# A gated mix of attention and FFN: a new list of steps, which also says where each gelu tanh is queued

## The chip, the cores and the metric

The kernel runs on one core of a Trainium2 chip. The metric is the device time of one execution, in microseconds. Before the change the median of three runs is 1306.47 us (1300.94 to 1306.64).

## What is computed

The reference takes 2048 tokens of 512 numbers and mixes two branches by a gate per token. One branch is attention with 32 query heads of size 16 over a single key and value head; the other is an FFN with a gelu gate and 1376 hidden columns.

```python
q = (x @ wq) as 32 heads of 16;  k = x @ wk;  v = x @ wv
p = softmax(q @ k.T * 16 ** -0.5)            # per head, 2048 x 2048
a = (p @ v, heads side by side) @ wo
b = (gelu(x @ w_gate) * (x @ w_up)) @ w_down # gelu by the tanh formula
g = sigmoid((x * gate_w).sum(-1))
out = g * a + (1 - g) * b
```

All is in float32. The FFN, the projections and `wo` are computed with each operand split into a rounded high part and the rest (`split`, L196), in three products; scores take both parts of q and k side by side in 51 rows.

## The kernel before

A prologue of some 80 us loads x and the weights, projects q, k and v and writes q to DRAM in a layout that is read back by head. The rest, over nine tenths of the time, is one long list of steps for TensorE, in which attention and FFN are interleaved, and this list is written out by hand or by a planner as `PLAN` (L44): 78 lines of letters, each with a count behind it.

- **S**, a score (`scores`, L724): for a group of queries and 128 keys, two matmuls (L738) that run side by side in the two halves of the array's rows write 128 x 1024 scores into a pair of PSUM banks, and ScalarE takes the exponential of it all into a buffer `p` in SBUF (L741). There are three such bank pairs (`two_banks`, L137). S takes the one of the first two that has been unused for longer; **Z** is a score that takes the third. There are 1024 S and Z in all.
- **V**, a visit (`visit`, L818, and `pv`, L802): four matmuls (L808; eight records in a profile) multiply the two oldest pairs of `p` with v and add to an accumulator in one PSUM bank. After 16 V's the accumulator is full: VectorE copies it out (`norm`, L744, the copies are L752 and L762), which frees the bank, and the later steps of the norm are put on a list `bg` of small VectorE work. There are 512 V's.
- **H** and **F**, a job of the FFN or of `wo`: H opens the job. It takes the third bank pair for its result `z` and a bank of its own for `y`; an **F** is one pair of matmuls (L503), one for z and one for y, again in the two halves of the array's rows (`pair_mm`, L497). A job goes through its terms twice, the second time with the halves exchanged; between the two stands a small instruction on POOL, `mark` (L511), for which the second half waits. A gate job (`gate_job`, L562) computes a chunk of 128 hidden columns of gate (z) and up (y) for 512 tokens, in 24 F's; a down job (`down_job`, L590) multiplies two or three finished chunks with `w_down`, adding z and y to the output (L608, L610); a `wo` job does the same for the attention's result. Every third F (`slot`, L477) also issues one small piece of work from the lists `todo` (splits of the next weights: a cast on VectorE, L200, and a subtraction on POOL, L201), `lazy` and `bg`.
- **R** ends the job (`end`).

What follows a gate job is a chain of four links (`gelu`, L524): VectorE copies z out (`gs`, L528), then *inner*, two VectorE operations (L531, L532) that make the tanh's argument `sq`; *tanh* on ScalarE (L535); *outer* (L538, L539), two VectorE operations, the second of which reads y; *halves* (L543, L544), which split the result into `hh` and `hl` for the down job. The copy and *inner* are issued at R. The other links wait on the list `chain`, and `advance(m)` (L549) issues links until only m are left. Every engine works through its own queue in order, so a link that is issued early stands in front of what is issued later on the same engine, whether its input is there or not.

Before the change four things issue the links: the job's `end` puts them off by a number of scores (`defer`, L295, counts S and Z as they are issued; `run_later`, L655, is called by each of them ahead of its own matmuls), tanh by 3, outer by 5, halves by 6; H issues up to outer, as its y needs the old bank; the next gate job's `gelu` issues all that is left; and `ffn_jobs` (L635) issues all of it before it hands out the first down job of a batch, because that job reads `hh` and `hl`:

```python
            if r % 3 == 2 or r == NF - 1:
                flush(chain)
                batch = hold[:]
```

`play` (L827) is called for each line of the list with the next job of its kind. A job's `begin` is called first, then the letters are played one by one. `begin` of a gate job also issues the load of the weights two chunks on (`fetch_w`, L298), flushes `todo` and puts off the splits of the next chunk's weights by two scores. There are 39 gate jobs in the list, 32 down jobs in 16 batches and six `wo` jobs, with 1608 F's.

## Time and profile before

| | |
|---|---|
| median of three runs | 1306.47 us |
| the profiled execution's own time | 1303.09 us |
| its span, first to last instruction | 1301.3 us |
| mean granted TensorE clock | 0.991 |
| TensorE busy | 1260.4 us (97%) |
| ScalarE busy | 1033.5 us (79%) |
| VectorE busy | 559.7 us (43%) |
| POOL busy | 222.9 us (17%) |
| exponentials on ScalarE | 1024, 979.6 us |
| tanhs of the gelu, 128 x 512 | 40, 25.0 us |

PE is TensorE, PEld its loading of weights, DVE VectorE, ACT ScalarE. A row of a timeline gives the start in us from the span's start, the duration, the engine, the line, the operation, the tiles (written <- read), the shapes and how many equal instructions are merged; in brackets stands idle time ahead of it and what ended that. A row of the waits gives who waited for whom, the us in total, how often and the longest. Since matmuls are pipelined and overlap, their price is read from start to start.

### The profile page before, as it was taken

The page shows a single profiled execution, that of the slowest core. Times are in us where ns is not written, and L with a number is a line of the kernel's source. Part 1 is how long each engine was busy: PE and PEld are TensorE (multiplying, and loading weights), DVE is VectorE, ACT ScalarE, POOL GpSimd, SP SyncE. Part 2 cuts the span into 40 slices and gives each one's busy share as a digit, 9 for nine tenths or more (in the row PEclk, how much of TensorE's full clock was granted, in tenths as well). Part 3 has the DMA queues.
Part 4 walks back from the last instruction along what each step waited for, and adds up shares of the span by engine and source line. Part 5 has one row for each costly group of instructions (what it writes and reads, how often), then busy time and mean ns, then how long its engine had stood idle before and what let it go on. Part 6 is the DMA issues. An engine that isn't in the chain of part 4 may idle for free.

```text
span 1301.3 us, 23608 instructions
## 1 busy us (share of the span) xinstructions
PE 1260.4 (97%) x9742; PEld 653.5 (50%) x9742; DVE 559.7 (43%) x843; ACT 1033.5 (79%) x1126; POOL 222.9 (17%) x264
## 2 busy tenths in 40 slices
PE   9989999999999999999999999999999999999998
PEld 6865545454545545544454544444544554454545
DVE  6872543525523352533453244261555225254334
ACT  4547888787888888878888878897888789788884
POOL 4420312112300210202230021120231012021100
PEclk9999999999999999999999999999999999999999
DMA  8550201012200211101210211010221201011000
GB/s 315 186 176 19 79 25 59 17 46 78 70 14 18 79 38 38 63 22 38 98 38 14 71 62 38 17 60 1 73 85 38 70 14 62 25 39 38 14 1 33
DMA packets 28173, 73.89 MB, mean 57 GB/s; under 512 B 4192, under 2 KB 4192, under 8 KB 28064
## 3 DMA queue, kind: packets, MB, share of 16 engines
q1 hardware_dynamic: 27520, 71.06, 16.4%
q8 instruction: 77, 1.26, 0.4%
q0 software_dynamic: 256, 0.79, 0.2%
q10 hardware_dynamic: 288, 0.52, 0.1%
q14 instruction: 32, 0.26, 0.1%
HBM read 57.41 MB, written 14.94 MB: 56 GB/s over the span
## 4 chain that ended last, share of the span: by engine, by line
PE 88%; DVE 4%; ACT 1%; issue 1%; DMA 0%; ACTq 0%; SPq 0%; DVEq 0%
PE acc L808 36%; PE s L738 22%; PE z L503 16%; PE y L503 14%; ACT p L741 1%; DVE sq L531 1%; DVE sq L532 1%; DVE gs L528 1%; PE wos L488 1%; DVE gs L539 0%; DVE sq L538 0%; DMA Q<-scr 0%; DVE acc L620 0%; DVE nz L774 0%; ACT sq L535 0%
## 5 line engine op out<-in xcount | busy, mean ns | idle before, releaser
L741 ACT ACTIVATE p<-s 128x1024 f32<-128x1024 f32 x1024 | 979.6, 1025 | 184.3 <-PE s L738 169.4
L808 PE MATMUL acc<-p,v 128*32 128x512 f32 x4096 | 505.8, 610 | 0.0
L738 PE MATMUL s<-Q,kp 51*128 51x512 f32 x2048 | 408.7, 426 | 27.1 <-ACT p L741 25.6
L738 PEld LDWEIGHTS s<-Q,kp 51*128 51x128 f32 x2048 | 187.6, 185 | 292.6 <-ACT p L741 191.8
L808 PEld LDWEIGHTS acc<-p,v 128*32 128x32 f32 x4096 | 109.0, 110 | 236.0 <-issue 228.0
L201 POOL TENSOR_TENSOR gl<-st,gh 128x512 fp32r<-128x512 f32 x80 | 113.8, 1439 | 334.4 <-PE s L738 159.6
L503 PE MATMUL y<-xh,gh 64*128 64x512 f32 x312 | 123.5, 396 | 5.5 <-DVE gs L539 5.4
L528 DVE COPY gs<-z 128x512 f32<-128x512 f32 x39 | 27.0, 691 | 231.6 <-PE z L503 179.0
L503 PE MATMUL z<-xh,gh 64*128 64x512 f32 x312 | 123.0, 394 | 0.3 <-ACT p L741 0.3
L503 PE MATMUL z<-xl,gh 64*128 64x512 f32 x312 | 122.3, 392 | 0.0
L503 PE MATMUL y<-xl,gh 64*128 64x512 f32 x312 | 122.1, 391 | 0.0
L503 PE MATMUL z<-xh,gl 64*128 64x512 f32 x312 | 122.0, 391 | 0.0
L503 PE MATMUL y<-xh,gl 64*128 64x512 f32 x312 | 121.9, 391 | 0.0
L511 POOL MEMSET mark<- 1x1 f32 x77 | 9.0, 117 | 629.8 <-PE y L503 613.4
L610 DVE SCALAR_TENSOR_TENSOR acc<-z,gc,acc 128x512 f32<-128x512 f32 x24 | 18.0, 751 | 165.5 <-PE z L503 114.7
L503 PE MATMUL y<-dh,hh 64*128 64x512 f32 x176 | 71.5, 406 | 0.0
L503 PE MATMUL z<-dh,hh 64*128 64x512 f32 x176 | 71.5, 406 | 0.0
L503 PE MATMUL z<-dl,hh 64*128 64x512 f32 x176 | 68.8, 391 | 0.0
L503 PE MATMUL y<-dl,hh 64*128 64x512 f32 x176 | 68.8, 391 | 0.0
L503 PE MATMUL z<-dh,hl 64*128 64x512 f32 x176 | 68.8, 391 | 0.0
L503 PE MATMUL y<-dh,hl 64*128 64x512 f32 x176 | 68.8, 391 | 0.0
L201 POOL TENSOR_TENSOR dl<-st,dh 128x512 fp32r<-128x512 f32 x44 | 58.3, 1325 | 54.2 <-DVE dh L200 51.9
(167 smaller groups left out, 1576.1 us busy)
## 6 DMA issues: line engine op xcount, KB each, us to landing
st<-wf SPq DMA_DIRECT2D x40, 768.0 KB
scr<-q SPq DMA_DIRECT2D x16, 512.0 KB
Q<-scr SPq DMA_DIRECT2D x64, 128.0 KB
Q<-scr SPq DMA_DIRECT2D x64, 64.0 KB
out<-acc SPq DMA_DIRECT2D x16, 256.0 KB
xr<-xT SPq DMA_DIRECT2D x6, 512.0 KB
xst<-xT SPq DMA_DIRECT2D x12, 256.0 KB
xr<-xT SPq DMA_DIRECT2D x4, 256.0 KB
```

The costliest lines, as they stand in the source:

```text
L201: eng_l.tensor_sub(lo, src, hi)
L488: nc.tensor.matmul(ps, a, b, start=(first and q == 0), stop=(last and q == len(terms) - 1), skip_group_check=True)
L503: mm = nc.tensor.matmul(ps, a[rs], b[rs], start=(half == 0 and q == 0), stop=(half == 1 and q == len(X) - 1), skip_group_check=True)
L511: relay = nc.gpsimd.memset(mark, 0.0).ins
L528: nc.vector.tensor_copy(gs, g)
L531: nc.vector.scalar_tensor_tensor(sq, gs, GC, gs, op0=ALU.mult, op1=ALU.mult)
L532: nc.vector.scalar_tensor_tensor(sq, sq, 1.0, gs, op0=ALU.add, op1=ALU.mult)
L610: nc.vector.scalar_tensor_tensor(o, ps, w, o, op0=ALU.mult, op1=ALU.add)
L738: nc.tensor.matmul(ps[:, j * TG : (j + 1) * TG], kp[rs, kc * P : (kc + 1) * P], Q[u][rs, pr], start=True, stop=True)
L741: nc.scalar.activation(p, ps, AF.Exp, bias=0.0, scale=SCALE)
L808: nc.tensor.matmul(accp[u][32 * j : 32 * j + 32], vt[:, kc], pb[s, j // 2][:, (j % 2) * TG : (j % 2 + 1) * TG], start=(kc == 0), stop=(kc ...
```

## The change

The list has a new letter, T, and is a new list. T issues a gate job's tanh where it stands, and puts off outer and halves by two and three scores from there; the job's `end` no longer puts off anything. And each line of the list now begins at H: what stood at the head of a line of before, the scores and visits between one job and the next, now stands at the end of the line of the earlier job, behind its R. So `begin` of a job, and the flush of the chain ahead of a first down job, are played after the scores and visits of the gap, no longer ahead of them. The list holds the same 1024 scores (120 in the third bank pair, 111 before), 512 V's, 77 jobs and 1608 F's; its V's stand in 278 groups instead of 268. Nothing else in the kernel is changed.

```diff
 PLAN = [
-    "f: S2 H F5 S F5 S F2 S V S F2 S F3 S F5 S F2 R",
-    "f: S V S Z S V3 S Z S V2 H F S F3 S F3 S F2 S V S F3 S F5 S2 F R",
...
+    "t: S",
+    "f: H F S F5 S F4 S F2 S V S F2 S F4 S F4 S F2 R S V Z S T S V3 S Z S V2 S",
...
@@ -577,8 +577,6 @@
         def end(z, y):
             gelu(n, z, lambda: y)
             advance(3)()
-            for k, m in ((3, 2), (5, 1), (6, 0)):
-                defer(k, advance(m))
             if r == NF - 1:
                 flush(todo)
                 fetch_w(n + 3)
@@ -834,6 +832,10 @@
                     score(t[0] == "Z")
             elif t[0] == "V":
                 visit(k)
+            elif t[0] == "T":
+                advance(2)()
+                for k, m in ((2, 1), (3, 0)):
+                    defer(k, advance(m))
             elif t[0] == "H":
                 advance(1)()
                 z = two_banks("z", 2)[:, 0:TG]
```

The first place is on ScalarE, from the tanh of gate job 6 to the scores behind the one of gate job 8 (`sq` is the tile that a tanh turns into its result, `p` the output of an exponential). Before:

```order
L535 ACTIVATE sq_2491<-sq_2491 128x512
L741 ACTIVATE p<-s 128x1024 x15
L535 ACTIVATE sq_2669<-sq_2669 128x512
L741 ACTIVATE p<-s 128x1024 x14
L535 ACTIVATE sq_2870<-sq_2870 128x512
L741 ACTIVATE p<-s 128x1024 x40
```

And now:

```order
L535 ACTIVATE sq_2487<-sq_2487 128x512
L739 ACTIVATE p<-s 128x1024 x14
L535 ACTIVATE sq_2664<-sq_2664 128x512
L739 ACTIVATE p<-s 128x1024 x16
L535 ACTIVATE sq_2865<-sq_2865 128x512
L739 ACTIVATE p<-s 128x1024 x37
```

The third tanh of each piece is that of gate job 8, which a down job follows. 125 exponentials of the list stand ahead of the second tanh in both. Job 8's last score is the 139th of the list before and the 138th now; its tanh stood right behind the 139th exponential and now stands behind the 141st, three past the job's last score. Over all 39 gate jobs, 15 tanhs stood with no exponential between the job's last score and them, and 24 with two; now 32 stand with three, three with two and four with one, each of the four behind a group of three V's.

The second place is on TensorE, from the end of gate job 12 to the start of gate job 13 (`acc` rows are V's, 4 matmuls each, `s` rows scores, 2 matmuls each). Before:

```order
L503 MATMUL y<-xh_3605,gl_3349 128x512
L738 MATMUL s<-Q_3140,kp 128x512 x2
L808 MATMUL acc_3589<-p,v_75 32x512 x4
L738 MATMUL s<-Q_3140,kp 128x512 x4
L738 MATMUL s<-Q_3577,kp 128x512 x2
L808 MATMUL acc_3589<-p,v_75 32x512 x16
L738 MATMUL s<-Q_3577,kp 128x512 x4
L503 MATMUL z<-xh_3605,gh_3742 128x512
```

And now:

```order
L503 MATMUL y<-xh_3629,gl_3417 128x512
L736 MATMUL s<-Q_3542,kp 128x512 x2
L806 MATMUL acc_3604<-p,v_75 32x512 x4
L736 MATMUL s<-Q_3542,kp 128x512 x4
L806 MATMUL acc_3604<-p,v_75 32x512 x8
L736 MATMUL s<-Q_3542,kp 128x512 x6
L806 MATMUL acc_3972<-p,v_76 32x512 x8
L736 MATMUL s<-Q_3542,kp 128x512 x2
L503 MATMUL z<-xh_3629,gh_3813 128x512
```

Before, the last V's of an accumulator stood directly ahead of the two scores and the job; now they stand earlier, and three scores, two V's of the next accumulator and one more score come between them and the job.

The third place is on POOL, over the gate jobs 6 and 7 (`gl` and `dl` are subtractions of the next weights' splits, `mark` stands between a job's halves; the first `mark` of the piece of now belongs to two down jobs and gate job 6). Before:

```order
L511 MEMSET mark 1x1 x2
L201 TENSOR_TENSOR gl_2342<-st_1868,gh_2341 128x512 x2
L511 MEMSET mark 1x1
L201 TENSOR_TENSOR dl_2340<-st_1868,dh_2339 128x512
L201 TENSOR_TENSOR gl_2513<-st_2324,gh_2512 128x512 x2
L511 MEMSET mark 1x1
```

And now:

```order
L511 MEMSET mark 1x1 x3
L201 TENSOR_TENSOR gl_2420<-st_1964,gh_2419 128x512 x2
L201 TENSOR_TENSOR dl_2418<-st_1964,dh_2417 128x512
L511 MEMSET mark 1x1
L201 TENSOR_TENSOR gl_2576<-st_2386,gh_2575 128x512 x2
L201 TENSOR_TENSOR dl_2574<-st_2386,dh_2573 128x512
```

Two of a job's three subtractions stood ahead of its `mark` and one behind it; now all three stand behind it.

## The prediction

> **What bounds the kernel now.** I read the page first: how busy each engine is, and the chain that ended last.

> ```profile
> PE 1260.4 (97%) x9742; PEld 653.5 (50%) x9742; DVE 559.7 (43%) x843; ACT 1033.5 (79%) x1126; POOL 222.9 (17%) x264
> ...
> PE 88%; DVE 4%; ACT 1%; issue 1%; DMA 0%; ACTq 0%; SPq 0%; DVEq 0%
> ```

> TensorE is the bound, and DMA is nothing. A list that only reorders its work can change two things: what a step costs by what stands beside it, and where TensorE waits. So I read TensorE's timeline for the prices of the steps. In these rows `acc` x8 is one V, `s` x2 one score, a z and a y row one F.

> ```profile
> 110.48 0.68 PE L738 MATMUL s<-Q,kp 51*128 51x512 f32 x4
> 111.00 0.40 PE L503 MATMUL y<-dh,hl 64*128 64x512 f32 x1
> 111.00 0.40 PE L503 MATMUL z<-dh,hl 64*128 64x512 f32 x1
> 111.33 1.93 PE L808 MATMUL acc<-p,v 128*32 128x512 f32 x16
> 113.18 0.97 PE L738 MATMUL s<-Q,kp 51*128 51x512 f32 x6
> 114.08 2.78 PE L808 MATMUL acc<-p,v 128*32 128x512 f32 x24
> 116.80 0.50 PE L738 MATMUL s<-Q,kp 51*128 51x512 f32 x2
> 117.13 0.39 PE L503 MATMUL z<-dh,hh 64*128 64x512 f32 x1
> ```

> ```profile
> 127.67 0.39 PE L503 MATMUL z<-xl,gh 64*128 64x512 f32 x1
> 127.68 0.39 PE L503 MATMUL y<-xl,gh 64*128 64x512 f32 x1
> 127.91 0.45 PE L738 MATMUL s<-Q,kp 51*128 51x512 f32 x2
> 128.20 0.39 PE L503 MATMUL z<-xh,gl 64*128 64x512 f32 x1
> ```

> By starts, an F or a score takes 0.23 to 0.24 us (127.67 to 127.91). A group of V's costs more at its ends: 0.33 from the F at 111.00 to the first V, 1.85 for two V's (114.08 to 116.80 is 2.72 for three, so one more V is 0.87 and 0.11 goes at the end), and 0.33 for the first score behind (116.80 to 117.13). That is 0.10 + 0.11 + 0.10 = 0.31 a group. Laid on the whole list of before, such prices give 1136.1 us for the 1202.0 us from the first score at 82.8 to the last V at 1284.9. The other 66 us are waits, matmuls at a lower clock and scatter, and the rest of this part finds them. TensorE's own waits:

> ```profile
> PE s L738 <- ACT p L741: 25.6, 16, 1.9
> PE y L503 <- DVE gs L539: 7.1, 5, 1.7
> ```

> Scores wait 16 times for an exponential, nearly always 1.9 us. On ScalarE stands the cause:

> ```profile
> ACT sq L535 <- DVE sq L532: 24.8, 15, 1.9
> ```

> Fifteen of 39 gelu tanhs reach ScalarE's queue before their input is there. The gap after gate job 8, on TensorE, VectorE and ScalarE:

> ```profile
> 246.02 0.40 PE L738 MATMUL s<-Q,kp 51*128 51x512 f32 x2
> 246.35 1.07 PE L808 MATMUL acc<-p,v 128*32 128x512 f32 x8
> 247.35 0.73 PE L738 MATMUL s<-Q,kp 51*128 51x512 f32 x4
> 249.99 0.64 PE L738 MATMUL s<-Q,kp 51*128 51x512 f32 x2 [1.92 <-ACT p L741]
> ```

> ```profile
> 246.22 0.69 DVE L528 COPY gs<-z 128x512 f32<-128x512 f32 x1 [2.35 <-PE z L503]
> 246.95 0.69 DVE L531 SCALAR_TENSOR_TENSOR sq<-gs 128x512 f32<-128x512 f32 x1
> 247.67 0.69 DVE L532 SCALAR_TENSOR_TENSOR sq<-sq,gs 128x512 f32<-128x512 f32 x1
> ```

> ```profile
> 245.53 1.02 ACT L741 ACTIVATE p<-s 128x1024 f32<-128x1024 f32 x1
> 248.40 0.63 ACT L535 ACTIVATE sq<-sq 128x512 f32<-128x512 f32 x1 [1.85 <-DVE sq L532]
> 248.94 2.83 ACT L741 ACTIVATE p<-s 128x1024 f32<-128x1024 f32 x3
> ```

> The tanh can run at 248.40 at the earliest, but stands ahead of the exponential of the score of 246.02. ScalarE stands still for 1.85 us with three scores ready, no score bank comes free, and the score due at 247.9 (0.33 and 0.23 behind 247.35) starts at 249.99. It loses 2.08 us: 1.92 of waiting and 0.16 because its weights are no longer loaded in advance.

> A second loss follows it. The first row is the whole span's, the others give, for a stretch, its length, TensorE's busy time, the granted clock and the DMA:

> ```profile
> core 0: 1301.3 us, clock 0.991
> ```

> ```profile
> 246.00:256.00 10.00, 8.08 (x52) 0.83 0.00 0
> 559.00:569.00 10.00, 8.08 (x54) 0.83 0.00 1
> ```

> ```profile
> 256.00:559.00 303.00, 296.63 (x2404) 1.00 0.15 48
> ```

> Seven windows of 10 us (from 92, 246, 559, 680, 795, 883 and 1112) have 0.83 or so, and each holds one of those waits; between them the clock is 1.00. Each loses 0.17 of 10 us, 1.7 us. Seven make 11.9 us, and 0.009 of 1301.3 us is 11.7.

> The five waits of `y` are of another kind; here is the start of gate job 13, on VectorE and on TensorE:

> ```profile
> 351.69 0.69 DVE L752 COPY n<-acc 128x512 f32<-128x512 f32 x1 [2.59 <-PE acc L808]
> 352.30 0.68 DVE L538 SCALAR_TENSOR_TENSOR sq<-sq,gs 128x512 f32<-128x512 f32 x1
> 353.01 0.69 DVE L539 SCALAR_TENSOR_TENSOR gs<-y,sq 128x512 f32<-128x512 f32 x1
> ```

> ```profile
> 351.55 0.74 PE L738 MATMUL s<-Q,kp 51*128 51x512 f32 x4
> 352.13 0.39 PE L503 MATMUL z<-xh,gh 64*128 64x512 f32 x1
> 353.76 0.50 PE L503 MATMUL y<-xh,gh 64*128 64x512 f32 x1 [1.24 <-DVE gs L539]
> ```

> The old `y` bank is read by L539, which is queued on VectorE behind the copy of a finished accumulator, and that copy waits for the V's just ahead of the job. From 352.13 to 353.76 an F takes 1.63 instead of 0.23.

> **The change, part by part.** The sum is made against the profiled execution, 1303.1 us (span 1301.3, 1.8 around it); the median of the three timed runs, 1306.5, is 0.3% above it.

> *Where the tanh stands.* Counted in the lists and ScalarE's order, 15 tanhs of before have no exponential between the job's last score and themselves (all where a down job follows, so the chain was finished early), and 24 have two. Those 24 do not wait. Now 32 have three, three have two and four have one. In job 8's gap the first exponential can start at 246.42, when its score ends, and three at 0.94 (2.83 for three) end past 249.2; the input is ready at 248.40. The four with one follow a group of three V's: the tanh may wait, but the next score comes only some 3.3 us after the job's last F (0.23 + 0.33 + 2.7), and VectorE's chain ends 2.6 us after it (246.02 less 0.23, to 248.40). So all 15 stalls go: 25.6 of waiting and 15 times 0.16, **-28.0**.

> *The low clock.* If the stalls cause it, **-11.9**. The row first: idle of 1.92 us was enough seven times in 15. [...]

> *The `y` waits.* L538 and L539 now come two scores behind the tanh, and the list keeps at least two V's between them, or the accumulator's copy, and the next job. Two V's and their ends are some 2.1 us, the two operations 1.4. All five go: 7.1 and five times 0.16, **-7.9**.

> *Late scores.* The score at 127.91 is followed 0.29 later, not 0.23: its bank came free just too late to load weights in advance. In the whole timeline 148 of 3,129 steps are 0.04 to 0.20 late, 10.9 us in sum (the first at 83.2, the last at 1269.6). ScalarE gives an exponential per 0.94 us. By the prices, 110 scores of before start less than 2.7 us after the third score before them (third-bank scores left aside), and 11 of the new list. The ends are 0 and 10.9; I take **-8.0**, as nine tenths of the tight places go but not every late step need be one.

> *More groups of V's.* 278 against 268: ten times 0.31, **+3.1**. Every kind of matmul keeps its number.

> *What moves along, at nothing.* A job's `begin` is played at H now, no longer at the end of the job before, so its weight fetch (SP), its splits (VectorE, POOL) and the flush of `todo` come later in their queues. The fetched weights are split one job later, over 10 us on; VectorE is 43% busy and runs ahead of TensorE. On POOL three subtractions stand behind a job's `mark` where two stood ahead of it; their end is due 4 to 5 us after the job's middle, about when the job ends. If that cover fails, a chain meets them: the second rival. The loads of Q hang on scores and do not move.

> The sum: 1303.1 - 28.0 - 11.9 - 7.9 - 8.0 + 3.1 = 1250.4, rounded up to **1251 us**.

> **The rivals.** *The low-clock windows stay.* [...] Against it: the places above. 1251 + 11.9 = 1263; chance 0.07.

> *POOL holds up the gelu chain.* One row of the view of the tile `sq` (shortest, median and longest duration) speaks for it:

> ```profile
> L532 DVE SCALAR_TENSOR_TENSOR sq<-sq,gs x40: 691/692/1632, 81.8 to 1259.1; 128x512 f32<-128x512 f32 x40
> ```

> The one of 1632 ns ran against a POOL subtraction, 0.94 us too long. [...] If the later subtractions hit every chain, a tanh behind three exponentials still has its input about in time; the seven with fewer lose up to 0.94 each, 6.6 us: 1257; chance 0.08.

> *ScalarE is too tight.* With the stalls gone the same 1024 exponentials must fit in 50 us less, and the late scores stay: 1251 + 8 = 1259; chance 0.07.

> *The far side: every gate job waits for `y`.* What five jobs paid, 39 could pay, if L539, now fixed two scores behind a later tanh, came after the next H. 34 more at 1.58 us (7.9 / 5) are 53.7; with the 7.9 that then stay: 1250.4 + 61.6 = 1312, slower by 0.4% than the median and 0.7% than the profiled run. It decides where less than 1.4 us of TensorE's work lies between that place and H; I find no such gap in the list. 0.02, with 0.01 more for a partial case near no change.

> **How the numbers follow.** My case has 0.75. It is the likeliest, so 1251. Its own range is 1246 (every late step goes, 1247.5, and a little scatter) to 1257. The range reaches up over the POOL and ScalarE rivals to the low-clock windows: 1246 to 1264. About 0.5% is what a measurement of this kernel can tell from no change, 6.5 us; all cases but the last are faster by far more: 0.97, 0.01, 0.02.

> **What would show it.** In the profile of the changed kernel the wait of `sq` L535 for L532 falls from 24.8 us to under 4, TensorE's wait for `p` from 25.6 to under 3 and for L539 from 7.1 to under 1, the mean clock rises to 0.998 or more, and the page's TensorE share to 98%. A clock still at 0.991 without long waits shows the first rival; L531 or L532 medians above 692 ns the second; many waits of weight loads for `p` the third. A time above 1275 means that a wait took another's place, and my reading of the gaps is wrong.

## The result, and the profile after

| | before | after |
|---|---|---|
| median | 1306.49 us (four runs, 1300.94 to 1306.64) | 1252.9 us (four runs, 1252.69 to 1253.59) |
| the profiled execution's own time | 1303.09 us | 1252.75 us |
| its span | 1301.3 us | 1250.9 us |

The changed kernel takes 0.9601 of the time of before (95% interval 0.9575 to 0.9626). 1251.0 was predicted, 1246 to 1264 as the range.

The page of the changed kernel: how busy each engine is, and the chain that ended last. Line numbers between a gate job's `end` (L580) and the new letter in `play` are lower by two than before: L741 is L739 now, L738 is L736, L808 is L806.

```profile
PE 1239.9 (99%) x9742; PEld 657.1 (53%) x9742; DVE 519.3 (42%) x843; ACT 1032.1 (83%) x1126; POOL 214.2 (17%) x264
...
PE 92%; DVE 1%; DMA 0%; ACT 0%; issue 0%; SPq 0%; DVEq 0%
```

```profile
core 0: 1250.9 us, clock 0.999
```

TensorE went from 97% to 99% busy, with 20.5 us less of busy time for the same 9742 matmuls; about half of that is the low clock (seven stretches of 3.41 us at half clock before, one now), which the next section prices. Its longest waits now:

```profile
PE z L503 <- DVE oh L780: 3.9, 1, 3.9
PE pw L213 <- DVE kmx L214: 1.2, 1, 1.2
```

The 25.6 us for exponentials and the 7.1 us for L539 are gone from the list altogether, and at its head stands a wait that the kernel before did not have. On ScalarE the tanhs' wait fell from 24.8 us to this:

```profile
ACT sq L535 <- DVE sq L532: 3.2, 4, 1.3
```

The gap after gate job 8 once more, on VectorE, ScalarE and TensorE. It ran from 246.02 before and runs from 238.17 now:

```profile
239.82 0.69 DVE L532 SCALAR_TENSOR_TENSOR sq<-sq,gs 128x512 f32<-128x512 f32 x1
```

```profile
240.09 1.94 ACT L739 ACTIVATE p<-s 128x1024 f32<-128x1024 f32 x2 [0.41 <-PE s L736]
241.91 0.63 ACT L535 ACTIVATE sq<-sq 128x512 f32<-128x512 f32 x1
242.43 2.85 ACT L739 ACTIVATE p<-s 128x1024 f32<-128x1024 f32 x3
```

```profile
239.49 0.97 PE L736 MATMUL s<-Q,kp 51*128 51x512 f32 x6
240.38 1.92 PE L806 MATMUL acc<-p,v 128*32 128x512 f32 x16
242.24 0.73 PE L736 MATMUL s<-Q,kp 51*128 51x512 f32 x4
```

The tanh's input is ready at 240.51 (239.82 and 0.69), 2.34 us after the first score behind the job (238.17); before it was 2.34 us too (246.02 to 248.36). But now ScalarE is still at the exponentials that stand ahead of the tanh, until 241.91, so it waits for nothing, and TensorE has no idle time in the whole gap. VectorE does the same work at the same speed, 0.69 us for L528, L531 and L532 each. TensorE's order of scores and V's is the same up to the fourth score, the one that waited before, but for the bank pairs of the second and the third. What differs is the place of one 0.63 us instruction in ScalarE's queue.

### The profile page after: what moved, and what is told of

Read it like the earlier page. It is cut to its first block, busy times and chain, and to the rows that moved or that the text cites. A ratio compares the mean times of both kernels' runs of the same rounds, so it can differ in the third digit from the quotient of the medians.

```text
span 1250.9 us, 23613 instructions
## 1 busy us (share of the span) xinstructions
PE 1239.9 (99%) x9742; PEld 657.1 (53%) x9742; DVE 519.3 (42%) x843; ACT 1032.1 (83%) x1126; POOL 214.2 (17%) x264
## 4 chain that ended last, share of the span: by engine, by line
PE 92%; DVE 1%; DMA 0%; ACT 0%; issue 0%; SPq 0%; DVEq 0%
PE acc L806 38%; PE s L736 23%; PE y L503 16%; PE z L503 14%; PE wos L488 1%; DVE nz L772 0%; DVE acc L618 0%; DMA Q<-scr 0%; PE wof L488 0%; DVE sq L531 0%; DVE n L763 0%; DVE sq L532 0%; DVE nt L775 0%; DVE gs L539 0%; DVE sq L538 0%; DVE hl L544 0%
## 5 line engine op out<-in xcount | busy, mean ns | idle before, releaser
L739 ACT ACTIVATE p<-s 128x1024 f32<-128x1024 f32 x1024 | 979.3, 1025 | 156.9 <-PE s L736 149.9
L806 PE MATMUL acc<-p,v 128*32 128x512 f32 x4096 | 497.7, 600 | 0.0
L736 PE MATMUL s<-Q,kp 51*128 51x512 f32 x2048 | 396.4, 421 | 0.8 <-DMA Q<-scr 0.8
L736 PEld LDWEIGHTS s<-Q,kp 51*128 51x128 f32 x2048 | 183.1, 184 | 258.9 <-ACT p L739 157.5
L806 PEld LDWEIGHTS acc<-p,v 128*32 128x32 f32 x4096 | 107.2, 109 | 236.5 <-issue 224.5
L528 DVE COPY gs<-z 128x512 f32<-128x512 f32 x39 | 27.0, 691 | 251.2 <-PE z L503 229.7
L503 PE MATMUL z<-xh,gh 64*128 64x512 f32 x312 | 123.2, 395 | 0.0
L503 PE MATMUL y<-xh,gh 64*128 64x512 f32 x312 | 123.1, 394 | 0.0
L503 PE MATMUL y<-xl,gh 64*128 64x512 f32 x312 | 121.9, 391 | 0.0
L503 PE MATMUL y<-xh,gl 64*128 64x512 f32 x312 | 121.9, 391 | 0.0
L503 PE MATMUL z<-xh,gl 64*128 64x512 f32 x312 | 121.9, 391 | 0.0
L503 PE MATMUL z<-xl,gh 64*128 64x512 f32 x312 | 121.9, 391 | 0.0
L201 POOL TENSOR_TENSOR gl<-st,gh 128x512 fp32r<-128x512 f32 x80 | 106.9, 1354 | 63.4 <-DVE gh L200 51.2
L503 PE MATMUL y<-dh,hh 64*128 64x512 f32 x176 | 69.4, 395 | 0.0
L503 PE MATMUL z<-dh,hh 64*128 64x512 f32 x176 | 69.4, 395 | 0.0
L503 PE MATMUL y<-dl,hh 64*128 64x512 f32 x176 | 68.8, 391 | 0.0
L503 PE MATMUL y<-dh,hl 64*128 64x512 f32 x176 | 68.8, 391 | 0.0
L503 PE MATMUL z<-dh,hl 64*128 64x512 f32 x176 | 68.8, 391 | 0.0
L503 PE MATMUL z<-dl,hh 64*128 64x512 f32 x176 | 68.8, 391 | 0.0
L503 PEld LDWEIGHTS z<-xh,gh 64*128 64x128 f32 x312 | 58.0, 186 | 8.3 <-ACT p L739 1.7
```

The costliest lines, as they stand in the source:

```text
L201: eng_l.tensor_sub(lo, src, hi)
L503: mm = nc.tensor.matmul(ps, a[rs], b[rs], start=(half == 0 and q == 0), stop=(half == 1 and q == len(X) - 1), skip_group_check=True)
L528: nc.vector.tensor_copy(gs, g)
L736: nc.tensor.matmul(ps[:, j * TG : (j + 1) * TG], kp[rs, kc * P : (kc + 1) * P], Q[u][rs, pr], start=True, stop=True)
L739: nc.scalar.activation(p, ps, AF.Exp, bias=0.0, scale=SCALE)
L806: nc.tensor.matmul(accp[u][32 * j : 32 * j + 32], vt[:, kc], pb[s, j // 2][:, (j % 2) * TG : (j % 2 + 1) * TG], start=(kc == 0), stop=(kc ...
```

## Where the 50 us came from

I laid the price of each step (the prediction's 0.23 for an F or a score, 0.87 and 0.31 for V's) beside its measured length, from the start of one step of TensorE to the next, for every step of the main loop, in both profiled executions. What exceeds the price by 0.04 to 0.20 us is called late, by more long. The prices in the sums have more digits than these: with the printed ones all steps come to 1133 and 1136 us, some 3 us less in each kernel.

| us | before | after |
|---|---|---|
| prices of all steps | 1136.1 | 1139.4 |
| late steps | 161, 12.2 | 23, 2.0 |
| long steps | 42, 48.6 | 4, 5.4 |
| the rest (scatter) | 4.7 | 5.0 |
| main loop | 1202.0 | 1152.2 |

The 48.6 of before part into 27.8 at the 15 tanh stalls, 11.5 in the low clock behind them, 7.9 at the five waits for `y`, and 1.4 elsewhere. The 5.4 of after stand at one place, the new wait. The loop gives 49.8 us of the 50.3, the prologue and the end the other 0.5.

## Experiments

**The theories.** Mine is the prediction's: the gain is made by where a tanh, its followers and the flush ahead of a down job stand in their queues, 28 us directly and 12 through the clock, and late scores and V groups belong to the list's order. The rivals: the gain comes from the new order of scores and visits as such (more even for ScalarE), with the stalls only a symptom; or the stalls and the low clock are separate losses. Each expectation below gives the numbers of the theories for that run.

**The old list, cut at H.** The list of before, its lines cut anew so that each begins at H (the first lines of the edit). Not one score, visit or F changes place on TensorE; what changes is when `begin` and the flush of the chain are played. The delays are the old 3, 5 and 6.

```diff
-    "f: S2 H F5 S F5 S F2 S V S F2 S F3 S F5 S F2 R",
-    "f: S V S Z S V3 S Z S V2 H F S F3 S F3 S F2 S V S F3 S F5 S2 F R",
+    "t: S2",
+    "f: H F5 S F5 S F2 S V S F2 S F3 S F5 S F2 R S V S Z S V3 S Z S V2",
...
```

> The old list, only cut anew: each line begins at H, so no chain is finished early; links are put off by 3, 5 and 6 scores as before. Theory A (the tanh's place makes the long waits, and these make the low clock): all 39 tanhs stand behind two exponentials, ScalarE's wait for L532 falls from 24.8 us to under 2, the mean clock rises from 0.991 to 0.998 or more; the waits for y grow from 7.9 to about 13 us, since outer is now 5 scores late ahead of down jobs too: 1303.1 - 28.0 - 11.9 + 5 = 1268 us. Rival B (the gain is the new list's mix of steps): above 1295. Rival C (the low clock has another cause): clock still 0.991, about 1280.

Measured: 1266.86 us (ratio 0.9708, 0.9685 to 0.9730). The profiled execution's cores and TensorE's longest wait:

```profile
core 0: 1265.8 us, clock 0.998
```

```profile
PE y L503 <- DVE gs L539: 8.9, 7, 1.7
```

No tanh waits any more, and the clock went from 0.991 to 0.998 with them, at TensorE's old order and the old prices (1136.1). The cut alone gives 38 us (against the runs of before beside it, median 1304.67), where the change gave 54 against its own; by the ratios, 2.9% of 4.0%. The late steps hardly moved (149, 11.0 us), and the waits for `y` went from 7.1 to 8.9 us, less than I had expected. That rules out the order of scores and visits as the cause of the stalls.

**The same, with outer one score earlier.** To see whether the `y` waits are a term of their own:

```diff
-            for k, m in ((3, 2), (5, 1), (6, 0)):
+            for k, m in ((3, 2), (4, 1), (6, 0)):
```

> As e1_rotate, with outer put off by 4 scores instead of 5. Theory A: the y waits fall to some 2 us, the small late starts of the old list stay (10.9 us): 1303.1 - 28.0 - 11.9 - 6 = 1257 us, with over 100 late steps left. Rival (late starts were a consequence of the long waits): they go too, 1247 us.

Measured: 1255.34 us (ratio 0.9623, 0.9601 to 0.9644).

```profile
core 0: 1253.6 us, clock 0.999
```

```profile
PE y L503 <- DVE gs L539: 0.5, 1, 0.5
```

Seven waits became one short one, and 11.5 us went, 3.1 more than the 8.4 us of waiting. By my estimate the clock makes some 1.3 of it (0.998 against 0.999 in the two profiled runs, 0.001 of 1265.8 us), and 1.1 is the 0.16 us that the wait after gate job 8 of before lost on top of its 1.92, taken seven times; the rest stays unexplained. With one digit changed the old order of TensorE's work reaches within 2.4 us of the new list. 142 late steps, 10.5 us, are still there, now that hardly a stall is left: they belong to the old list's order, not to the stalls.

**The new list, with the old delays.** The other half: the new list without its T's, and tanh, outer and halves put off by 3, 5 and 6 scores in `end`, as before.

> The new list without T: the tanh, outer and halves are put off by 3, 5 and 6 scores from the job's end, as before the change. Theory A: two exponentials ahead of a tanh are enough, so no long waits; outer comes up to one score later than now and a few y waits return, about 4 us: 1253 + 4 = 1257 us. Rival (the third exponential ahead of the tanh is what matters): tens of tanh waits on ScalarE, 1275 us or more.

```diff
-    "f: H F S F5 S F4 S F2 S V S F2 S F4 S F4 S F2 R S V Z S T S V3 S Z S V2 S",
+    "f: H F S F5 S F4 S F2 S V S F2 S F4 S F4 S F2 R S V Z S S V3 S Z S V2 S",
...
             advance(3)()
+            for k, m in ((3, 2), (5, 1), (6, 0)):
+                defer(k, advance(m))
```

Measured: 1260.36 us (ratio 0.9665, 0.9642 to 0.9688).

```profile
PE z L503 <- DVE oh L782: 3.8, 1, 3.8
PE y L503 <- DVE gs L539: 1.7, 1, 1.7
PE s L738 <- ACT p L741: 1.4, 5, 0.3
```

Again no tanh waits: the letter T is not what frees them, the cut is. T is worth 7 us here (10.0 us of long steps against 5.4, 37 late steps against 23). I had put it 3 us too low. In place of 4 us at waits for `y` the profile has 1.9 at one such wait, 1.7 at five short waits for `p`, which I had not counted, and 1.6 more of late steps than the changed kernel.

**The changed kernel, with the early flush put back.** The gate job's `end` issues the whole chain at once where a down job follows, as before; all else is the changed kernel.

```diff
             advance(3)()
+            if r % 3 == 2 or r == NF - 1:
+                flush(chain)
```

> The new kernel, but the chain of a gate job that a down job follows is issued whole at R, as before the change; T stays for the others. Theory A: 15 or 16 tanhs wait on ScalarE again, about 25 us there; TensorE loses 22 to 28 us in scores and up to 12 by the lower clock: 1253 + 22 to 40 = 1275 to 1293 us, clock 0.991 to 0.995. Rival B (the new list is what counts): below 1262. Rival C (the clock does not follow the waits): clock 0.999.

Measured: 1284.61 us (1283.03 to 1288.53; ratio 0.9843, 0.9819 to 0.9867).

```profile
core 0: 1286.7 us, clock 0.991
```

```profile
PE s L738 <- ACT p L741: 21.8, 17, 2.3
```

```profile
ACT sq L535 <- DVE sq L532: 27.6, 16, 2.2
```

The gap after gate job 8, on ScalarE:

```profile
243.83 0.63 ACT L535 ACTIVATE sq<-sq 128x512 f32<-128x512 f32 x1 [1.79 <-DVE sq L532]
```

Everything came back that was said to go: the tanhs' waits, the scores' waits behind them, and the low clock. The 0.991 is that of the profiled run, the slowest of the four; the others have 0.993 to 0.995, still below the changed kernel's 0.999. From before over the changed kernel to this one the low clock went and came with the stalls: 0.991 where the tanhs wait 24.8 us, 0.999 where they wait 3.2, 0.991 again where they wait 27.6. The time lies 32 us above the changed kernel, and the late steps (39, 3.8 us) did not come back.

**One exponential between.** The same, but the chain put off by two scores instead of issued at once, so that one exponential or so comes between the job's last score and the tanh:

```diff
             advance(3)()
+            if r % 3 == 2 or r == NF - 1:
+                defer(2, advance(0))
```

> The new kernel, but in gate jobs that a down job follows the tanh is issued with the second score behind R, so that one exponential stands between. Theory A: ScalarE waits some 0.7 to 0.9 us in each of about 15 places, 12 to 15 us in all, but most of it is covered, since a score bank is free: TensorE loses about 3 us, the clock stays at 0.999: 1256 us. Rival (each wait of ScalarE costs TensorE about what it cost before): 1270 us or more.

Measured: 1257.82 us (ratio 0.9655, 0.9636 to 0.9673).

```profile
core 0: 1256.1 us, clock 0.997
```

```profile
ACT sq L535 <- DVE sq L532: 12.5, 15, 1.3
```

Fifteen tanhs still wait, 12.5 us in all against 27.6, but that costs only 5 us against the changed kernel: with one exponential more ahead of the tanh, ScalarE's stall of 0.8 us (12.5 in 15) mostly ends before TensorE needs a bank (its waits for `p` are 2.0 us in all). So ScalarE's 0.8 us of standing still cost TensorE little here, while with its stalls of 1.7 us in the kernel above (27.6 in 16) TensorE waited 21.8 us in all. (Outer and halves are also issued right behind the tanh in this kernel, not two and three scores later; no run tells what that alone does.) The clock I had expected at 0.999; the rest of this is below, under the clock.

**Outer and halves left to the next H.** This kernel tests the far side of the prediction: T issues the tanh and puts off nothing, so L538 and L539 come when the next H, or the next chain, asks for them.

```diff
                 advance(2)()
-                for k, m in ((2, 1), (3, 0)):
-                    defer(k, advance(m))
```

> The new kernel, but outer and halves are not put off from T: outer is issued at the next H and halves with the next flush. Far-side theory of the prediction: every gate job's y is waited for, 39 places at 1.58 us: about 1315 us. Theory A: the place in the program is not a time; VectorE reaches outer as soon as what stands ahead of it is done, so y is waited for only where an accumulator's copy stands ahead, about 10 places at 1.4 to 2 us: 1253 + 18 = 1271 us.

Measured: 1284.7 us (1281.01 to 1288.03; ratio 0.9867, 0.9844 to 0.9890).

```profile
PE y L503 <- DVE gs L539: 20.2, 11, 5.4
```

Eleven jobs wait, not 39. At 26 of the 39 gate jobs L538 starts 0.03 us behind its tanh: it stands later in the list, but nothing stands ahead of it on VectorE. In ten of the eleven that wait, the copy of a finished accumulator stands directly ahead of it, as here, where the tanh had ended at 153.67; in the eleventh it is the end of a norm.

```profile
157.12 0.69 DVE L760 COPY n<-acc 128x512 f32<-128x512 f32 x1 [5.49 <-PE acc L806]
157.72 0.68 DVE L538 SCALAR_TENSOR_TENSOR sq<-sq,gs 128x512 f32<-128x512 f32 x1
158.44 0.69 DVE L539 SCALAR_TENSOR_TENSOR gs<-y,sq 128x512 f32<-128x512 f32 x1
```

The number of waits is the one that I had expected, but I had put the time 13 us too low. In the profiled run, the fastest of the four (1281.01), the eleven steps lose 22.0 us (one of them 5.6, at the same `wo` job as the new wait below), 17.9 more than that wait costs the changed kernel: as I had put it. What I had left out are steps at the half clock behind three of the waits, 5.4 us (the clock of this run is 0.994), two other long steps of 3.0 us together, and 38 late steps outside the low clock, 3.7 us.

**The new wait taken away.** The wait of 3.9 us stands at a `wo` job. VectorE's and TensorE's rows there, of the changed kernel:

```profile
948.15 0.69 DVE L760 COPY n<-acc 128x512 f32<-128x512 f32 x1 [7.61 <-PE acc L806]
...
957.29 0.69 DVE L544 TENSOR_TENSOR hl<-gs,hh 128x512 fp32r<-128x512 f32 x1
957.90 0.74 DVE L766 SCALAR_TENSOR_TENSOR nz<-n,mk,nz 128x512 f32<-128x512 f32 x1
...
960.00 3.39 DVE L772 RECIPROCAL nz<-n 128x128 f32<-128x128 f32 x4
...
964.15 0.43 DVE L780 CAST oh<-nt 128x512 fp32r<-128x512 f32 x1
```

```profile
960.29 0.40 PE L503 MATMUL z<-woh,ol 64*128 64x512 f32 x1
960.29 0.40 PE L503 MATMUL y<-woh,ol 64*128 64x512 f32 x1
964.63 0.78 PE L503 MATMUL z<-woh,oh 64*128 64x512 f32 x1 [3.94 <-DVE oh L780]
```

The last accumulator of a group of tokens is copied out at 948.15, in the middle of a gate job. What remains of its norm (L766 to L784) is on the list `bg`, but the job's later slots go to weight splits, and the `begin` of the `wo` job flushes what is left. That `begin` is now played at H, where the last link of the gelu chain has already been issued (957.29), and 6.7 us of norm work lie between 957.90 and the end of the cast at 964.58, for which the job's term with the last heads waits until 964.63. The chain ahead of it was itself held up a little, by 0.4 us: L531 took 1.11 us there instead of 0.69, while a POOL subtraction ran.

```profile
952.05 1.28 POOL L201 TENSOR_TENSOR dl<-st,dh 128x512 fp32r<-128x512 f32 x1
952.77 1.11 DVE L531 SCALAR_TENSOR_TENSOR sq<-gs 128x512 f32<-128x512 f32 x1
```

Before, the same flush was played at the R of the gate job:

```profile
1003.83 2.56 DVE L774 RECIPROCAL nz<-n 128x128 f32<-128x128 f32 x3
...
1007.16 0.43 DVE L782 CAST oh<-nt 128x512 fp32r<-128x512 f32 x1
...
1009.02 0.69 DVE L539 SCALAR_TENSOR_TENSOR gs<-y,sq 128x512 f32<-128x512 f32 x1
```

There the rest of the norm stood ahead of L538 and L539, and one of the five waits for `y` was this one (to 1009.76). The experiment plays the two down jobs that follow first, and the two `wo` jobs after them; one V moves from one line to another, so that an accumulator still ends with its group of V's:

```diff
-    "w: H F4 S F4 S F2 S F2 V S F2 S F4 S F4 S F2 R S V S Z S V3 S Z S V3 S",
-    "w: H F S F5 S F3 S F3 S V3 S F2 S F4 S F4 S F2 R S V2 S2",
     "f: H F6 S F3 S V S F2 S F4 S F3 R S V Z S2 V3 S",
-    "f: H F S F7 S F S V S F3 S F3 S F3 R S V Z S2 V3 Z S2 V2 S",
+    "f: H F S F7 S F S V S F3 S F3 S F3 R S V Z S2 V2 Z S2 V2 S",
+    "w: H F4 S F4 S F2 S F2 V2 S F2 S F4 S F4 S F2 R S V S Z S V3 S Z S V3 S",
+    "w: H F S F5 S F3 S F3 S V3 S F2 S F4 S F4 S F2 R S V2 S2",
```

> The new kernel with the two wo jobs of the third token group moved behind the two down jobs that followed them, and one V moved across a gap so that an accumulator still ends with its group. Theory A: the 3.9 us wait of TensorE for oh L780 near 960 us goes, with the stretch at the lower clock behind it, 5.4 us in all; a gap of the new order costs some 0.5 back: 1253 - 5 = 1248 us, clock 1.000 or close. Rival (VectorE's norm holds up some other job there): the wait appears under another name, 1252 or more.

Measured: 1247.99 us (five runs, 1247.85 to 1248.28; ratio 0.9577, 0.9562 to 0.9592). In the profile no wait for `oh` is left, the conversion comes at 968.48, and ahead of it the two down jobs have work:

```profile
core 0: 1245.9 us, clock 1.000
```

```profile
968.48 0.43 DVE L780 CAST oh<-nt 128x512 fp32r<-128x512 f32 x1
```

Long steps fell from 5.4 to 0.4 us, prices and late steps stayed as they were (1139.4; 23, 2.0 us). The two kernels were not timed side by side, and their ratios to before overlap, since before itself scatters; but no run of this one comes within 4 us of a run of the changed kernel, and the profiles differ by just the wait and the steps at half clock behind it. This list beats the changed kernel, by some 5 us by the times and the profiles (3 by the ratios).

## Why the prediction was right

By its terms, in us:

| term | predicted | measured |
|---|---|---|
| 15 tanh stalls | -28.0 | -27.8 |
| low clock behind them | -11.9 | -11.5 |
| five waits for `y` | -7.9 | -7.9 |
| late scores | -8.0 | -10.2 |
| ten more groups of V's | +3.1 | +3.3 |
| what moves along | 0 | +5.4 |
| the rest, not foreseen | 0 | -1.4 at other long steps, +0.3 scatter, -0.5 outside the loop |

- *The tanh.* Right in size and mechanism. The 25.6 us that went into the sum hold one wait of 0.3 us that follows no tanh, and twelve of the 16 waits, not nearly all, are 1.9 us; the sum hardly suffers. The four tanhs with one exponential ahead of them wait 3.2 us in all, and TensorE loses nothing at three of them (the fourth is at the new wait). One thing is shifted: I tied the gain to the tanh's place in the new list, three exponentials behind. The old list with the new cut shows that taking the chain's early flush away is enough, and the early flush in the new list brings the stalls back. T itself is worth some 7 us, by keeping tanh, outer and halves clear of short waits.
- *The low clock.* It went with the stalls (0.999) and returned with them (0.991 with the early flush). The rival that the low-clock windows stay (1263) is out.
- *The `y` waits.* Gone, as said; one digit in the old list takes most of them too.
- *Late scores.* 10.2 of 12.2 us went, 2.2 more than I took. I had counted only the late steps that a score begins, 10.9 of the 12.2. That ScalarE would be too tight (1259) is out: the late steps fell from 161 to 23 with ScalarE busier, 83% against 79%. The waits of weight loads for `p`:

```profile
PEld s L736 <- ACT p L739: 157.5, 202, 0.8
```

  Before, it was 191.8 us in 335 waits.
- *POOL.* The rival's mark does not show. Shortest, median and longest of the two VectorE operations of *inner*:

```profile
L531 DVE SCALAR_TENSOR_TENSOR sq<-gs x40: 687/692/1110, 81.2 to 1208.3; 128x512 f32<-128x512 f32 x40
L532 DVE SCALAR_TENSOR_TENSOR sq<-sq,gs x40: 691/693/1648, 81.9 to 1209.0; 128x512 f32<-128x512 f32 x40
```

  The medians are where they were, 692 and 693 ns. In three of the 40 chains L531 took 1.06 to 1.11 us while a subtraction ran, where before its longest was 0.695; the one L532 of 1.65 us stands ahead of the main loop, as the one of 1.63 did before. The one place where that can have cost TensorE something is the new wait, where it put the norm back by 0.4 us.
- *The step that failed* is "What moves along, at nothing", in its sentence that the flush comes later in its queue and VectorE "is 43% busy and runs ahead of TensorE". I followed the weight splits, the loads and POOL past the new place of `begin`, but of the lists that a `begin` flushes only `todo`, and of the jobs only the gate jobs. A `wo` job's `begin` flushes `bg` as well, and once in the list that holds nearly 7 us of VectorE work that this very job reads. An average of 43% says nothing of a place where so much is due at once. This cost 5.4 us. The late scores gave back 2.2 of it and what I had not foreseen 1.6; with 0.8 on the other terms the sum of 1250.4 ends 2.4 lower than the measured 1252.75. That it came so near is luck: the misses cancel. The far-side price of 1312 could not be reached: without the delays 11 jobs wait, not 39.

## What to carry to other kernels

What an instruction costs in an in-order queue is what it holds up behind it, here a tanh of 0.63 us for which ScalarE stood still for 1.85 us with scores ready: place it so that work whose input is ready stands ahead of it for as long as its own input takes. When an edit moves the place where a list of put-off work is flushed, follow every list that is flushed there, for every kind of job, and ask how much can be on it at the worst place. And when stalls make the clock fall, that can add to their own price, here four tenths (11.5 us on 27.8).

## What the runs showed of the hardware

```profile
171.69:175.11 3.42, 1.75 (x15) 0.61 (x19) 2.55 (x6) 3.34 (x5) 0.00 (x0) 1.00 0.00 0
246.79:250.20 3.41, 1.49 (x14) 0.48 (x6) 2.54 (x5) 1.80 (x3) 0.00 (x0) 1.00 0.00 0
250.20:253.61 3.41, 3.41 (x18) 0.79 (x20) 3.34 (x6) 2.48 (x3) 0.00 (x0) 0.50 0.00 0
362.84:366.25 3.41, 2.42 (x20) 0.74 (x16) 2.08 (x4) 1.63 (x4) 0.00 (x0) 1.00 0.00 0
366.25:369.66 3.41, 2.48 (x22) 0.86 (x26) 2.50 (x4) 3.41 (x4) 0.00 (x0) 1.00 0.01 2
```

A stall of 1.92 us that falls whole into one piece (246.79) leaves TensorE busy for 1.49 us of it, and the next piece runs at the half clock. Where an edge parts the stall (362.84 and 366.25), both pieces stay above 2.4 us busy, and the clock stays at 1.00. The piece from 171.69 with 1.66 us idle has no low one behind it. Over the whole main loop of before, the low stretches follow idle times of 1.81 to 1.92 us, and no other piece exceeds 1.66; in the changed kernel, 3.36 us (the piece from 961.27) against 0.78 at most. So seven of the 15 stalls of before have a low stretch behind them and eight have none. In the kernel with the early flush, too, one wait of 1.92 us (to 245.42) has a clock of 0.85 behind it, over the 10 us from 246, and another (to 96.42) 1.00 over the 10 us from 92. That the place of a stall between two edges decides this is my estimate from these pieces: no run moves a stall alone, and none shows how much idle time it takes.

The kernels with many stalls scatter by 5 to 7 us from run to run, and the changed kernel by 0.9. The granted clock of every run is on record, and the scatter goes with it: of the runs of before beside the first experiments the fastest has 1301.15 us at 0.992 and the slowest 1306.73 at 0.988, and 0.004 of 1305 us is 5.2 of the 5.6. Why the clock differs from run to run was not shown, since only one run of each was profiled. The kernel with one exponential between has a clock of 0.997: 0.003 of its 1256.1 us is 3.8 us, near the 3.4 that two stretches of 3.41 us at half clock lose. Its waits for `p` are 0.7 us at most, so my estimate is that both stand behind its wait of 3.9 us at the `wo` job, behind which the changed kernel has one.
